# First expert of a fused attention and mixture kernel: its first 256 tokens in plain float32, weights unsplit

## The chip, the cores and the metric

One core of one Trainium2 chip runs the whole kernel in one launch. The metric is the device time of one execution in microseconds (us); a kernel's time is the median of its runs. The core has a matrix engine (TensorE, PE in the rows; PEld is its weight load), VectorE (DVE), ScalarE (ACT) and GpSimd (POOL); SyncE (SP) issues nearly all DMAs. Each engine works through its own queue in the order in which the program has it.

## The reference, cut to what matters

```python
# attention: q, k, v (2, 8, 576, 64); s (2, 8, 576)
scores = q @ k.T / 8;  bias = -(cum[:, None] - cum[None, :]),  cum = cumsum(max(s, 0))
attn = softmax(where(causal, -1e9, scores + min(bias, 0)))
x = (attn @ v), heads side by side             # 1152 tokens x 512
# four experts, every token goes through all of them
p = domain_probs / (domain_probs.sum(-1) + 1e-9)
x2 = sum over e of p[:, e] * (max(x @ w1[e], 0) @ w2[e])      # w1 512x1024, w2 1024x512
out = ((x2 @ w_a) * (x2 @ w_b)) @ w_out                        # 512 -> 1536 -> 512
```

All inputs and the output are float32.

## The kernel before

Products of two float32 matrices are made from halves: each operand is cut into a part hi in the engine's one-pass format (float32r) and a rest lo, and `mm3` (L260) adds hi*hi, hi*lo and lo*hi in three matmuls. So everything that goes into `mm3` has to be split first. For the weights `split_piece` (L194) does this: one DMA brings half a slab (128x1024, 512 KB) into one of three buffers called raw, one instruction copies it to wh, which rounds it, and two subtracts make wl. Two such pieces are a slab (a w1 or w2 block of 512x512), and an expert has four slabs: two of w1 and two of w2. The wh and wl of four slabs have a place at a time. `nsplit` counts pieces: for the first `NFIRST` = 4 the wh copy and both subtracts run on POOL; from the fifth on the wh copy runs on ACT (L220) and the subtracts (L222) alternate between POOL and DVE.

Attention runs in four groups of query rows. Group 0 is tokens 0 to 255 of the first batch, 8 heads of two 128-row tiles; its matmuls are plain float32 (L604, L692). The other groups use split halves. `attn_step` (L805) is a software pipeline over (head, tile): scores (L604, or L606 and L607), softmax (L617 on DVE, L632 on ACT), normalising (L644, on DVE for group 0 and on POOL later), transposing on PE (L655), copying the transposed tile from PSUM (L671 on ACT, from group 1 on also the rest el, L673 on DVE), attention times v (L692). For group 0 the result of two heads goes from PSUM straight to xh (ACT) and xl (DVE), L706.

The experts' products on tokens 0 to 767 stand beside the attention. `stages` (L865) holds expert 0 on the first 256 tokens, expert 1 on the same, then expert 1 on the next two blocks of 256. A stage has 8 first-layer units (12 matmuls of 256 columns, then relu to hh on ACT, L296, and the rest hl on DVE, L297) and 2 second-layer units (24 matmuls of 512 columns, then the weighted sum on DVE, L315 or L317). `advance` (L1096) paces attention steps against the estimated matmul time of the units, so that group 1 is done 15 us of estimate before the second stage ends. While group 0 runs, no product has begun; the loop at L1049 puts a weight step (one load, one split) after every second attention step. Everything after the attention (plain_stage, relu_stage, ab_stage) is not touched.

A scheduler puts the instructions of each engine in order. SP's order matters as well: a raw load waits there until its buffer is free, and whatever is queued behind it waits too, among it the key and query loads of the next heads (kr L558, qr L557, and kb L573, which sends a rounded key from ks back to another place).

```python
        else:                                             # split_piece, a slab's piece (L212)
            nsplit[0] += 1
            lo_eng = nc.gpsimd if nsplit[0] % 2 or nsplit[0] <= NFIRST else nc.vector
            two = slice(2 * j, 2 * j + 2)
            if nsplit[0] <= NFIRST:
                nc.gpsimd.tensor_scalar(                  # wh, L216
...
    while state["n"] < ends[0]:                           # L1049
        attn_step()
        if state["n"] > 3 and state["n"] % 2 == 0 and pieces:
            weight_step()
```

Of the kernel before, what the change touches and what calls it, by code (L numbers as in the profile page):

```python
# [8 lines left out]
F32 = mybir.dt.float32  # L9
F32R = mybir.dt.float32r  # L10
I32 = mybir.dt.int32
AF = mybir.ActivationFunctionType
ALU = mybir.AluOpType
# [32 lines left out]
NTT = NT // P  # L46
NT0 = 256

NFIRST = 4

LAG = 2

# [2 lines left out]
def fused_kernel(ctx, tc, qT, kT, v, s, dp, w1, w2, wa, wb, wo, out):  # L55
# [476 lines left out]
    first["v"] = vx[:, : H * 2 * D].rearrange("p (h c d) -> p h c d", h=H, c=2)  # L532
    NR = len(GROUPS) * H
    cum = vx[:NR, H * 2 * D :]
    ckr = slab.tile([P, 3 * S], F32R, tag="wh", name="ckr")
    ck3 = [ckr[:NR, j * S : j * S + S] for j in range(3)]

    def load_first(a, z, k_eng):
        for key, src, eng in (("q", qT, nc.sync), ("k", kT, k_eng)):
# [140 lines left out]
    def st_av(j):  # L680
        a = (j.h % 2) * D
        if j.gi == 0 and j.h % 2:
            ps = xpair[j.gi]
        else:
            ps = ps_a.tile([P, j.nr], F32, tag="av", name=f"av{j.nm}")
        mms = []
        for c in range(j.i1):
            o = max(0, j.tiles[c][1] - j.r0)
            for e in (j.eh, j.el) if j.gi else (j.eh,):
                mms.append((c, o, e))  # L690
        for m, (c, o, e) in enumerate(mms):
            ins = nc.tensor.matmul(  # L692
                ps[:, o:] if j.gi else ps[a : a + D, o:],
                lhsT=j.vs[:, c, :],
                rhs=e[:, c, o:],
                start=(m == 0),
                stop=(m == len(mms) - 1),
            )
        passed[-1].append(ins.ins.name)
        c = D - a  # L700
        t0 = j.b * S + j.r0
        x = slice(t0, t0 + j.nr)
        if j.gi == 0:
            xpair[j.gi] = ps
            if j.h % 2:
                split(xh[j.h // 2][:, x], xl[j.h // 2][:, x], ps, nc.vector)  # L706
            return
        if j.h % 2 == 0:
            xpair[j.gi] = (
                x_p.tile([P, j.nr], F32, tag="xs", name="xs"),  # L710
                x_p.tile([P, j.nr], F32, tag="xt", name="xt"),
            )
        xs, xt = xpair[j.gi]
        nc.scalar.activation(out=xt[a : a + D, :], in_=ps[c : c + D, :], func=AF.Copy)
        nc.vector.tensor_tensor(
            out=xs[a : a + D, :], in0=ps[a : a + D, :], in1=xt[a : a + D, :], op=ALU.add
        )
        if j.h % 2 == 1:
            split(xh[j.h // 2][:, x], xl[j.h // 2][:, x], xs, nc.gpsimd)
# [141 lines left out]
                queue((key, w), "slab", src[w])  # L861
        return ws

    halves = [queue_expert(ex) for ex in range(2)]
    stages = [(ex, halves[ex], *TURNS[0]) for ex in range(2)]  # L865
    stages += [(1, halves[1], *turn) for turn in TURNS[1:-1]]

    lasts = [(ex, m) for ex in (0, 2, 3) for m in range(2 * NPR)]
    for k, (ex, m) in enumerate(lasts):
# [16 lines left out]
    def pipelined(stages, last_ahead):  # L886

        units, pend = [], []
        for st, after in zip(stages, [*stages[1:], None]):
            if st is None:  # L890
                units += pend
                pend = []
                continue
            first_, second = st
            n = 1 if after or not last_ahead else len(first_)
            units += first_[:n] + pend + first_[n:]
            pend = second
        return units + pend

    def expert_stage(ex, ws, t0, t1):  # L900
        l1 = [
# [146 lines left out]

    while state["n"] < ends[0]:  # L1049
        attn_step()  # L1050
        if state["n"] > 3 and state["n"] % 2 == 0 and pieces:
            weight_step()

    def keys_of(k):
        return () if k is None else k if isinstance(k[0], tuple) else (k,)

    beside = pipelined([expert_stage(*st) for st in stages], False)
    after = pipelined(
        [plain_stage(w, m, *TURNS[-1]) for w in halves[1] for m in range(NPR)]
        + [relu_stage(ex, m) for ex, m in lasts]  # L1060
# [20 lines left out]
        area.append(area[-1] + (x[0].tiles[x[1]][0] + P if x else P))  # L1081

    turn_t = [0.0]
    for n in (2, 3, 4):
        us = sum(c for st in stages[:n] for part in expert_stage(*st) for _, c, _ in part)
        turn_t.append(us)
    SLACK = 15.0
    lead = []
    for g in range(3):
# [89 lines left out]
```

## Time and profile before

| | us |
|---|---|
| runs | 747.41, 751.63, 753.83 |
| median | 751.63 |
| the profiled execution's own time | 750.41 |
| its span, first to last instruction | 748.7 |
| mean granted TensorE clock | 0.990 of full speed |

The span is what the trace shows; the 1.7 us around it are the start and the end of the execution. Windows and start times count from the span's start. The profile gives the granted clock of PE as a share of 2.4 GHz, so 0.50 is the lower level, 1.2 GHz.

### The profile page before, as it was taken

To read this page: it belongs to the slowest core of one execution; us is meant where nothing else is said; L and a number is where in the kernel's file an instruction comes from. 1 tells how busy PE (TensorE), PEld (TensorE's weight loads), DVE (VectorE), ACT (ScalarE), POOL (GpSimd) and SP (SyncE) were. 2 spreads that over 40 slices of the span, in tenths; PEclk is the share of its full clock that TensorE was granted. 3 is DMA by queue.
4 is the path that set the end of the run, shared out by engine and by line. 5 is a ranking of instruction groups with operands and counts; after the bars stand their busy time and mean duration, and the time that the engine had idled before them with its cause. 6 is when DMAs were issued, how large, how long until landed. Compare 5 with 4: busy or idle time off the path is not lost.

```text
span 748.7 us, 11078 instructions
## 1 busy us (share of the span) xinstructions
PE 711.3 (95%) x3868; PEld 624.1 (83%) x3868; DVE 532.7 (71%) x1119; ACT 335.3 (45%) x756; POOL 413.4 (55%) x330
## 2 busy tenths in 40 slices
PE   5878889999999999999999999999899999999997
PEld 3567778898889888888888888887788888888886
DVE  7777688785777786666555656779783888877764
ACT  4577779986723432223231234333545434242410
POOL 1796676765513653333330356587468688798600
PEclk9889999999999999999999999999999999999999
DMA  6465523453220211111110113223013232223003
GB/s 182 158 211 175 148 73 104 110 139 92 55 85 29 85 56 57 57 56 57 57 39 18 57 57 85 65 77 111 28 43 99 59 90 79 85 72 97 1 1 127
DMA packets 35096, 61.34 MB, mean 82 GB/s; under 512 B 3473, under 2 KB 19377, under 8 KB 35041
## 3 DMA queue, kind: packets, MB, share of 16 engines
q1 hardware_dynamic: 34864, 60.50, 26.9%
q8 instruction: 31, 0.51, 0.3%
q14 instruction: 25, 0.20, 0.1%
q10 hardware_dynamic: 176, 0.14, 0.1%
HBM read 55.02 MB, written 2.58 MB: 77 GB/s over the span
## 4 chain that ended last, share of the span: by engine, by line
PE 59%; DVE 15%; POOL 9%; ACT 6%; issue 6%; DMA 4%; SPq 0%; POOLq 0%; ACTq 0%; DVEq 0%
PE ps L264 29%; PE psq L264 20%; PE pst L264 4%; POOL wl L76 3%; PE av L692 2%; PE tr L655 2%; DMA kr<-in_kT 2%; PE sc L604 1%; ACT e L632 1%; POOL tp L157 1%; DMA raw<-in_w 1%; DVE tp L169 1%; DVE tp L165 1%; DVE h2l L76 1%; ACT wh L220 1%
## 5 line engine op out<-in xcount | busy, mean ns | idle before, releaser
L264 PE MATMUL ps<-wh,h2h 128*128 128x512 f32 x332 | 130.6, 393 | 0.0
L264 PE MATMUL ps<-wl,h2h 128*128 128x512 f32 x332 | 129.6, 390 | 0.0
L76 POOL TENSOR_TENSOR wl<-raw,wh 128x1024 fp32r<-128x1024 f32 x24 | 58.2, 2434 | 128.3 <-ACT wh L75 97.9
L264 PE MATMUL ps<-wh,h2l 128*128 128x512 f32 x332 | 125.8, 392 | 0.8 <-DVE h2l L76 0.8
L317 DVE SCALAR_TENSOR_TENSOR acc<-ps,pr,acc 128x512 f32<-128x512 f32 x111 | 82.3, 745 | 40.4 <-PE ps L264 39.8
L264 PE MATMUL psq<-xh,wh 128*128 128x448 f32 (+1 forms) x224 | 81.6, 364 | 0.1
L264 PE MATMUL psq<-xl,wh 128*128 128x448 f32 (+1 forms) x224 | 81.2, 363 | 0.0
L264 PE MATMUL psq<-xh,wl 128*128 128x448 f32 (+1 forms) x224 | 81.2, 363 | 0.0
L264 PEld LDWEIGHTS ps<-wh,h2l 128*128 128x128 f32 x332 | 62.1, 188 | 14.8 <-DVE h2l L76 1.7
L264 PEld LDWEIGHTS ps<-wh,h2h 128*128 128x128 f32 x332 | 62.4, 188 | 11.8 <-ACT h2h L75 0.2
L328 ACT ACTIVATE h2h<-psq 128x448 fp32r<-128x448 f32 (+1 forms) x56 | 29.6, 532 | 93.9 <-PE psq L264 73.5
L264 PEld LDWEIGHTS ps<-wl,h2h 128*128 128x128 f32 x332 | 62.4, 188 | 11.1
L76 POOL TENSOR_TENSOR wl<-sums,wh 128x1024 fp32r<-128x1024 f32 x24 | 58.2, 2423 | 4.9 <-ACT wh L75 4.8
L75 ACT ACTIVATE wh<-raw 128x1024 fp32r<-128x1024 f32 x24 | 25.5, 1062 | 67.8 <-PE ps L264 51.7
L655 PE MATMUL tr<-ident,e 128*128 128x128 f32 x240 | 45.2, 289 | 11.0 <-DVE el L673 6.4
L264 PE MATMUL psq<-tqh,wh 128*128 128x448 f32 x144 | 52.9, 368 | 2.1 <-DVE u L415 1.3
L264 PE MATMUL psq<-tql,wh 128*128 128x448 f32 x144 | 52.6, 365 | 0.0
L264 PE MATMUL psq<-tqh,wl 128*128 128x448 f32 x144 | 52.5, 364 | 0.0
L644 POOL TENSOR_SCALAR e<-e,r 128x448 f32<-128x448 f32 (+4 forms) x64 | 37.9, 596 | 25.1 <-DVE r L643 23.1
L157 POOL TENSOR_SCALAR tp<-tp 128x512 f32<-128x512 f32 x24 | 47.3, 1988 | 6.5 <-ACT tp L156 6.5
L673 DVE TENSOR_TENSOR el<-tr,eh 128x512 fp32r<-128x512 f32 (+5 forms) x80 | 38.5, 483 | 16.1 <-ACT eh L671 15.4
L415 DVE TENSOR_TENSOR u<-psq,s 128x448 f32<-128x448 f32 x48 | 29.6, 618 | 28.4 <-PE psq L264 22.3
(174 smaller groups left out, 1963.3 us busy)
## 6 DMA issues: line engine op xcount, KB each, us to landing
raw<-in_w SPq DMA_DIRECT2D x40, 512.0 KB
raw<-in_wa SPq DMA_DIRECT2D x12, 512.0 KB
raw<-in_wb SPq DMA_DIRECT2D x12, 512.0 KB
raw<-in_wo SPq DMA_DIRECT2D x12, 512.0 KB
kr<-in_kT SPq DMA_DIRECT2D x16, 288.0 KB
vr<-in_v SPq DMA_DIRECT2D x16, 160.0 KB
kb<-ks SPq DMA_DIRECT2D x16, 144.0 KB
out<-acc SPq DMA_DIRECT2D x9, 256.0 KB
```

The costliest lines, as they stand in the source:

```text
L75: nc.scalar.activation(out=hi, in_=src, func=AF.Copy)
L76: lo_eng.tensor_tensor(out=lo, in0=src, in1=hi.bitcast(F32), op=ALU.subtract)
L157: nc.gpsimd.tensor_scalar(out=t.bitcast(F32), in0=t.bitcast(F32), scalar1=2.0**-15, scalar2=GMAX, op0=ALU.max, op1=ALU.min,)
L165: nc.vector.scalar_tensor_tensor(out=t, in0=lo, scalar=29, in1=t, op0=ALU.logical_shift_right, op1=ALU.bitwise_or,)
L264: ins = nc.tensor.matmul(ps, lhsT=l, rhs=r, start=first and k == 0, stop=last and k == 2, skip_group_check=more)
L317: nc.vector.scalar_tensor_tensor(out=dst, in0=ps, scalar=share, in1=dst, op0=ALU.mult, op1=ALU.add)
L328: nc.scalar.activation(out=hh, in_=src, func=AF.Relu)
L415: nc.vector.tensor_tensor(out=out, in0=a, in1=b, op=ALU.add)
L644: (nc.gpsimd if j.gi else nc.vector).tensor_scalar(out=t.e, in0=t.e, scalar1=r, scalar2=1.0, op0=ALU.mult, op1=ALU.mult)
L655: ins = nc.tensor.transpose(ps[:, c - c0, :], t.e[:, k0 : k0 + P], ident)
L673: nc.vector.tensor_tensor(out=j.el[:, c0:c1, x], in0=src, in1=hi.bitcast(F32), op=ALU.subtract)
L692: ins = nc.tensor.matmul(ps[:, o:] if j.gi else ps[a : a + D, o:], lhsT=j.vs[:, c, :], rhs=e[:, c, o:], start=(m == 0), stop=(m == len(mms ...
```

## The change

Expert 0's products on tokens 0 to 255 are no longer made from halves. `plain_expert` multiplies float32 by float32 in single matmuls (`mm1`): 8 first-layer units of 4 matmuls with 256 columns, and 2 second-layer units of 8 matmuls with 512. Its four weight blocks w32 are loaded as they are, after attention steps 4, 7, 11 and 15; each takes one place of the wh or wl kind, the two of w2 in places that others leave. x of group 0 is first copied by ACT from PSUM to x32, which lies in the buffer ckr, and split from there: xh on ACT, xl on POOL (DVE before). The relu of these units is one instruction, on ACT and DVE in turn, with no hl. The 8 pieces of expert 0's weights are not split any more. `NFIRST` is 0: the first pieces split are now expert 1's, with wh on ACT and the subtracts on POOL and DVE in turn. The pace counts 4 passes for a plain matmul, and the turns are counted without expert 0's old stage.

```diff
-NFIRST = 4
+NFIRST = 0
+
+W32_STEPS = (4, 7, 11, 15)
...
-    ckr = slab.tile([P, 3 * S], F32R, tag="wh", name="ckr")
-    ck3 = [ckr[:NR, j * S : j * S + S] for j in range(3)]
+    ckr = slab.tile([P, NC * SL], F32, tag="wh", name="ckr")
+    ck3 = [ckr[:NR, j * S : j * S + S].bitcast(F32R) for j in range(3)]
+    x32 = [ckr[:, o : o + NT0] for o in (3 * S, 0, NT0, 2 * NT0)]
+
+    w32 = {
+        (key, m): slab.tile([P, NC, SL], F32, tag=t, name="w32")
+        for key in ("w1", "w2") for m, t in enumerate(("wh", "wl"))
+    }
+
+    def load_w32(key, m):
+        src = {"w1": w1, "w2": w2}[key][m]
+        for two in (slice(0, 2), slice(2, 4)):
+            nc.sync.dma_start(out=w32[key, m][:, two, :], in_=src[:, two, :])
...
             if j.h % 2:
-                split(xh[j.h // 2][:, x], xl[j.h // 2][:, x], ps, nc.vector)
+                c_ = j.h // 2
+                nc.scalar.activation(out=x32[c_], in_=ps, func=AF.Copy)
+                split(xh[c_][:, x], xl[c_][:, x], x32[c_], nc.gpsimd)
...
-    halves = [queue_expert(ex) for ex in range(2)]
-    stages = [(ex, halves[ex], *TURNS[0]) for ex in range(2)]
-    stages += [(1, halves[1], *turn) for turn in TURNS[1:-1]]
+    halves = {1: queue_expert(1)}
+    stages = [(1, halves[1], *turn) for turn in TURNS[:-1]]
...
+    def mm1(ps, w, x, start, stop):
+        ins = nc.tensor.matmul(ps, lhsT=w, rhs=x, start=start, stop=stop)
...
+        if mixed:
+            mixed[0](4 * (x.shape[-1] / 2400 + 0.013))
+
+    def plain_expert():
+        h32 = {}
+        def first_(m, f):
+            ps = ps_m.tile([P, NT0], F32, tag="mm", name="ps1")
+            for c in range(NC):
+                mm1(ps, w32["w1", m][:, c, f * P : f * P + P], x32[c], c == 0, c == NC - 1)
+            h32[m, f] = h = pools["h"].tile([P, NT0], F32, tag="hh", name="h32")
+            if f % 2:
+                nc.vector.tensor_scalar(out=h, in0=ps, scalar1=0.0, scalar2=None, op0=ALU.max)
+            else:
+                nc.scalar.activation(out=h, in_=ps, func=AF.Relu)
+        def second(t):
+            ps = ps_m.tile([P, DM], F32, tag="mm", name="ps2")
+            for m in range(2):
+                for f in range(NF):
+                    mm1(ps, h32[m, f][:, t : t + P], w32["w2", m][:, f, :], m + f == 0, m == 1 and f == NF - 1)
+            add_share(ps, 0, t)
...
     while state["n"] < ends[0]:
         attn_step()
+        if state["n"] in W32_STEPS:
+            load_w32(*list(w32)[W32_STEPS.index(state["n"])])
...
-    beside = pipelined([expert_stage(*st) for st in stages], False)
+    beside = pipelined([plain_expert()] + [expert_stage(*st) for st in stages], False)
```

The line numbers of the changed program are 2 to 54 higher. Three places show how the order changes.

SP before, at the first weight loads: raw are pieces of expert 0's w1 (in_w1) and w2; qr, kr, kb, vr are loads of group 1's first heads, of which 0_2 is the first and 1_2 the second. Two more raw pieces of w1 stand ahead of these rows.

```order
L151 DMA raw_300<-in_w1 128x1024
L557 DMA qr0_0_2_389<-in_qT 128x384
L558 DMA kr0_0_2_390<-in_kT 128x576
L559 DMA kb0_0_2_391<-ckD_72 3x576
L559 DMA kb0_1_2_444<-ckD_72 3x576
L581 DMA vr0_0_2_464<-in_v 128x320
L151 DMA raw_340<-in_w1 128x1024
L557 DMA qr0_1_2_442<-in_qT 128x384
L573 DMA kb0_0_2_391<-ks0_0_2_435 64x576
L151 DMA raw_383<-in_w2 128x1024
L557 DMA qr0_2_2_500<-in_qT 128x384
L151 DMA raw_430<-in_w2 128x1024
```

SP of the change at the same place: w32_116 and w32_117 are the two halves of expert 0's w1; the raw pieces are now expert 1's.

```order
L550 DMA w32_116<-in_w1 128x1024 x2
L153 DMA raw_226<-in_w1 128x1024
L153 DMA raw_263<-in_w1 128x1024
L153 DMA raw_309<-in_w1 128x1024
L571 DMA qr0_0_2_401<-in_qT 128x384
L572 DMA kr0_0_2_402<-in_kT 128x576
L573 DMA kb0_0_2_403<-ckD_72 3x576
L573 DMA kb0_1_2_456<-ckD_72 3x576
L595 DMA vr0_0_2_476<-in_v 128x320
L550 DMA w32_117<-in_w1 128x1024 x2
L153 DMA raw_349<-in_w1 128x1024
L153 DMA raw_395<-in_w2 128x1024
```

The loads of the first head of group 1 now stand behind five pieces of 512 KB instead of three, and the second block of w1 comes straight behind them without a wait for a split. The two blocks of w2 are loaded much later, each into the place of a block of w1 that PE is done with.

ACT before, in the last heads of group 0: e0_5 to e0_7 are exponentials of heads 5 to 7, eh copies of transposed tiles, xh a result of group 0.

```order
L632 ACTIVATE e0_5_0_0_369,l_372<-e0_5_0_0_369,mn_370 128x128
L632 ACTIVATE e0_5_0_1_404,l_407<-e0_5_0_1_404,mn_405 128x256
L671 ACTIVATE eh0_4_0_379<-tr0_4_0_0_361 128x128
L567 ACTIVATE qh0_0_2_388<-qr0_0_2_389 128x384
L75 ACTIVATE xh_66<-av0_2_0_335 128x256
L632 ACTIVATE e0_6_0_0_419,l_422<-e0_6_0_0_419,mn_420 128x128
L671 ACTIVATE eh0_4_0_379<-tr0_4_0_1_395 128x2x128
L572 ACTIVATE ks0_0_2_435<-kr0_0_2_390 128x576
```

ACT of the change, from the same exponential on: wh_224 and wh_307 are slabs of expert 1, ckr_115 is x32.

```order
L646 ACTIVATE e0_5_0_0_380,l_383<-e0_5_0_0_380,mn_381 128x128
L222 ACTIVATE wh_224<-raw_226 128x1024
L646 ACTIVATE e0_5_0_1_416,l_419<-e0_5_0_1_416,mn_417 128x256
L685 ACTIVATE eh0_3_0_347<-tr0_3_0_1_354 128x2x128
L685 ACTIVATE eh0_4_0_391<-tr0_4_0_0_372 128x128
L646 ACTIVATE e0_6_0_0_431,l_434<-e0_6_0_0_431,mn_432 128x128
L222 ACTIVATE wh_224<-raw_263 128x1024
L646 ACTIVATE e0_6_0_1_469,l_472<-e0_6_0_1_469,mn_470 128x256
L721 ACTIVATE ckr_115<-av0_2_0_344 128x256
L685 ACTIVATE eh0_4_0_391<-tr0_4_0_1_407 128x2x128
L685 ACTIVATE eh0_5_0_440<-tr0_5_0_0_423 128x128
L222 ACTIVATE wh_307<-raw_309 128x1024
```

Three wh copies now stand between the exponentials of group 0; before, none did, since POOL made the first four.

DVE of the change, in heads 6 and 7 of group 0: the two subtracts of expert 1's second piece (wl_225) stand ahead of the normalising of head 6's second tile, e0_6_0_1; those of the fourth (wl_308) stand ahead of group 1's first softmax, e0_0_2_2. Before, DVE's first weight subtracts stood behind that softmax.

```order
L658 TENSOR_SCALAR e0_6_0_0_431<-e0_6_0_0_431,r_465 128x128
L645 TENSOR_SCALAR mn_532<-mn_532 128x1
L224 TENSOR_TENSOR wl_225<-raw_263,wh_224 128x512 x2
L654 TENSOR_SCALAR l_472<-l_472 128x1
L657 RECIPROCAL r_484<-l_472 128x1
L658 TENSOR_SCALAR e0_6_0_1_469<-e0_6_0_1_469,r_484 128x256
...
L658 TENSOR_SCALAR e0_7_0_1_531<-e0_7_0_1_531,r_548 128x256
L224 TENSOR_TENSOR wl_308<-raw_349,wh_307 128x512 x2
L582 SCALAR_TENSOR_TENSOR qb0_83<-qr0_1_2_454,qh0_1_2_453 64x384
L631 ISA e0_0_2_2_552,mn_553<-sc0_0_2_2_524,causal_82 128x320
```

DVE thus has two pairs of subtracts in or right behind group 0 that it did not have there, and fewer later.

PE's two orders are the same, buffer numbers aside, from just behind the scores of head 2's first tile in attention group 2 (sc_2_0_0, L606 and L607; the groups count from 0) to the end of the program: 3305 matmul instructions.

## Rows read from the trace of the kernel before

**Rows 1.** Windows: us of the stretch, busy us (instructions) by engine, granted clock, DMA share, GB/s.

```profile
0.00:36.20 36.20, 25.14 (x89) 15.44 (x89) 26.73 (x117) 17.76 (x58) 17.51 (x30) 0.92 0.54 164
36.20:98.50 62.30, 50.26 (x314) 45.27 (x313) 46.04 (x120) 48.77 (x127) 47.22 (x45) 0.94 0.56 170
98.50:122.00 23.50, 20.84 (x163) 19.51 (x163) 19.08 (x61) 18.58 (x60) 15.19 (x20) 1.00 0.34 95
122.00:748.70 626.70, 615.04 (x3307) 543.90 (x3306) 440.80 (x823) 250.19 (x512) 333.53 (x236) 1.00 0.23 68
```

**Rows 2.** Waits of PE from 0 to 140: us in total, times, longest.

```profile
PE sc L604 <- DMA ka<-va: 8.8, 1, 8.8
PE tr L655 <- DVE el L673: 6.0, 4, 2.0
PE sc L606 <- DVE mn L617: 3.0, 3, 1.5
PE sc L606 <- POOL ks L574: 2.6, 1, 2.6
PE sc L607 <- DMA kb<-ks: 1.3, 1, 1.3
```

**Rows 3.** Chain that ended last, 36 to 122, its shares by line.

```profile
by line: DMA raw<-in_w 10.8%; issue 10.4%; DMA kr<-in_kT 10.0%; PE ps L264 9.3%; ACT wh L220 8.1%; ACT e L632 6.4%; DVE wl L222 6.3%; PE av L692 4.4%; ACT eh L671 3.8%; POOL ks L574 3.5%; PE tr L655 3.5%; POOL wl L222 3.5%; DVE e L617 2.9%;
```

**Rows 4.** PE's timeline (start, us, instruction, count): plain float32 in group 0.

```profile
24.67 0.59 PE L604 MATMUL sc<-ka,qa 65*128 65x256 f32 x2
25.20 0.86 PE L692 MATMUL av<-eh,va 128*64 128x256 f32 x4
25.99 0.44 PE L655 MATMUL tr<-ident,e 128*128 128x128 f32 x2
```

**Rows 5.** Groups by shape of PE, 24.65 to 24.9: busy us, mean ns.

```profile
L604 PE MATMUL sc<-ka,qa 65*128 65x256 f32 x2 | 0.6, 378 | 0.0
```

**Rows 6.** PE's timeline: split products, 256 columns and 512 columns.

```profile
60.32 0.28 PE L264 MATMUL ps<-xh,wl 128*128 128x256 f32 x1
...
62.42 0.28 PE L264 MATMUL ps<-xh,wl 128*128 128x256 f32 x1
...
86.15 0.39 PE L264 MATMUL ps<-wl,hh 128*128 128x512 f32 x1
...
87.76 0.39 PE L264 MATMUL ps<-wh,hl 128*128 128x512 f32 x1
```

**Rows 7.** Instructions on raw, 0 to 122: ns min/median/max, first and last start.

```profile
L222 POOL TENSOR_TENSOR wl<-raw,wh x20: 1262/1334/1741, 20.0 to 100.2; 128x512 fp32r<-128x512 f32 x20
L220 ACT ACTIVATE wh<-raw x12: 1039/1051/1063, 36.6 to 102.0; 128x1024 fp32r<-128x1024 f32 x12
L222 DVE TENSOR_TENSOR wl<-raw,wh x12: 735/1406/1789, 38.7 to 103.8; 128x512 fp32r<-128x512 f32 x12
L216 POOL TENSOR_SCALAR wh<-raw x4: 1043/1048/1050, 18.9 to 31.4; 128x1024 fp32r<-128x1024 f32 x4
```

**Rows 8.** Groups of DVE and ACT from 0 to 122: rest and relu, busy us, mean ns.

```profile
L297 DVE SCALAR_TENSOR_TENSOR hl<-ps,hh 128x256 fp32r<-128x256 f32 x14 | 5.8, 412 | 1.1 <-ACT hh L296 0.9
L296 ACT ACTIVATE hh<-ps 128x256 fp32r<-128x256 f32 x14 | 5.2, 372 | 1.5 <-PE ps L264 1.5
```

**Rows 9.** Groups of POOL from 0 to 36.2, columns as in rows 8.

```profile
L222 POOL TENSOR_TENSOR wl<-raw,wh 128x512 fp32r<-128x512 f32 x6 | 7.9, 1338 | 0.1
```

**Rows 10.** DVE's timeline in group 0: the same normalising, POOL idle and POOL splitting.

```profile
18.04 0.35 DVE L644 TENSOR_SCALAR e<-e,r 128x256 f32<-128x256 f32 x1
...
30.23 1.25 DVE L644 TENSOR_SCALAR e<-e,r 128x256 f32<-128x256 f32 x1
```

**Rows 11.** Windows, columns as in rows 1: the last heads of group 0.

```profile
24.00:32.00 8.00, 6.32 (x31) 3.63 (x30) 7.47 (x30) 5.97 (x22) 7.83 (x7) 0.88 0.52 166
```

**Rows 12.** Instructions on kr up to 70, columns as in rows 7.

```profile
L572 ACT ACTIVATE ks<-kr x5: 672/683/687, 27.0 to 67.3; 128x576 fp32r<-128x576 f32 x5
```

**Rows 13.** Timeline of PE in head 1 of group 1: the longest wait there.

```profile
45.32 0.41 PE L606 MATMUL sc<-ks,qh 128*128 128x320 f32 x1 [2.60 <-POOL ks L574]
```

More of the change, by code (lines that the diff above doesn't have):

```diff
@@ L898, in pipelined @@
         return units + pend
+    def mm1(ps, w, x, start, stop):
+        ins = nc.tensor.matmul(ps, lhsT=w, rhs=x, start=start, stop=stop)
+        if len(passed) > LAG:
+            for name in passed[-1 - LAG]:
+                tc.add_manual_dep(ins.ins, name, NOSYNC, reason="the attention's pace")
+        if mixed:
[17 more added lines that the diff above has]
+            add_share(ps, 0, t)
+        T = 4 / 2400
+        l1 = [
+            (None, NC * (T * NT0 + 0.052), lambda m=m, f=f: first_(m, f)) for m in range(2) for f in range(NF)
+        ]
+        return l1, [(None, 2 * NF * (T * DM + 0.052), lambda t=t: second(t)) for t in range(0, NT0, P)]
     def expert_stage(ex, ws, t0, t1):
@@ L1083, in fused_kernel @@
     turn_t = [0.0]
-    for n in (2, 3, 4):
-        us = sum(c for st in stages[:n] for part in expert_stage(*st) for _, c, _ in part)
-        turn_t.append(us)
+    for n in (1, 2, 3):
+        parts = [*plain_expert(), *(part for st in stages[:n] for part in expert_stage(*st))]
+        turn_t.append(sum(c for part in parts for _, c, _ in part))
     SLACK = 15.0
```

## The prediction

> **What bounds the kernel now.** I read the busy time by stretch first, then PE's waits, then the chain of waits, then durations. In [rows 1] PE is busy 25.1 + 50.3 + 20.8 + 615.0 = 711.3 of 748.7 us, so PE bounds the kernel; the reader should see where the other 37.4 us lie: 11.1 before 36.2, 12.0 in the 62.3 us of expert 0's stage, 2.7 in the next 23.5, and 11.7 in all the 627 us behind. PE's order is the same in both programs from about 122 us on, so nothing behind that point has a reason to change: the change is decided in the first 122 us.
>
> Of the 25.8 us that PE waits there, 8.8 are for the operands of the first scores, which both programs need [rows 2]. The 14.7 us between 36.2 and 122 are mostly waits for DVE (rests of the transposed tiles 6.0, score buffers 3.0), POOL (2.6) and a key transfer (1.3). None is long, and no engine but PE is near full on average: DVE 46.0, ACT 48.8 and POOL 47.2 of 62.3. The chain tells what feeds the waits [rows 3]: of the 86 us from 36 to 122 its steps are raw loads 10.8%, wh copies 8.1%, subtracts on DVE 6.3% and on POOL 3.5%, together 28.7% or 24.7 us, and 10.0% are key loads, which stand on SP behind raw loads. PE's own products are 9.3%. So the splitting of expert weights sets the pace here, in queues that it shares with the attention. [Rows 13] is an example: PE waits 2.6 us for the rest of head 1's keys, which POOL makes after weight subtracts.
>
> **The change part by part.** *PE's products.* Taken away are 8 x 12 = 96 matmuls of 256 columns and 2 x 24 = 48 of 512. In [rows 6] 18 steps lie between 60.32 and 62.42, 0.117 us each, and seven between 86.15 and 87.76, 0.23 each: 96 x 0.117 + 48 x 0.23 = 11.2 + 11.0 = 22.2 us. Added are 32 plain matmuls of 256 columns and 16 of 512. A plain one is two records: two of 256 columns cover 0.59 us [rows 4] and are 0.378 long [rows 5], so the second starts 0.212 after the first. A product of 256 columns is then 0.425 us, and one of 512, with twice the columns, 0.85 (an estimate from this row): 32 x 0.425 + 16 x 0.85 = 13.6 + 13.6 = 27.2, **+5.0 us**. From above: the four records of 256 and 128 columns in [rows 4] take 25.20 to 25.99 = 0.79 where 1.5 x 0.425 = 0.64 would be due, 0.15 too much for two products; 0.075 on each of the 48 would be 3.6 more, +8.6. Those products have a pass of 128 columns; ours have none below 256, so I take the row of 256. From below: 0.212 is the spacing of passes without a gap, so nothing under +5.0 is left.
>
> *Splits that go.* Expert 0's four slabs were 8 of 16 pieces. From 36.2 to 122 the 12 wh copies on ACT [rows 7] fall to 4 (expert 1's third and fourth slab; the first two are now copied in group 0): 8 x 1.05 = 8.4 us less. DVE's 12 subtracts fall to 4, 8 x 1.4 = 11.2 less; POOL's 20 less the six before 36.2 [rows 9] fall from 14 to 4, 10 x 1.33 = 13.3 less. With the plain relu 8 rests on DVE and 4 relus on ACT go, and 4 plain ones on DVE come, at 0.41 and 0.37 us [rows 8]: 1.6 less on DVE, 1.5 on ACT. So DVE sheds 12.8 of 65.1 us (46.0 + 19.1), ACT 9.9 of 67.4, POOL 13.3 of 62.4. The 3.9 us of waits on keys should go, since the split in front of them is gone or earlier, and most of DVE's 9.0; PE also has 5 us more to do in the gaps. I take 10 of the 14.7 us as recovered: **-10 us**. The bounds are 0 (the waits are the softmax's own latency, and the new passes are laid beside them) and -14.7.
>
> *Splits that are moved into group 0.* ACT gets three wh ahead of the last exponentials, 3 x 1.05 = 3.2, and two copies to x32, 0.8 by the 256-column pass of [rows 8]. In 24 to 32 ACT has 8.0 - 6.0 = 2.0 us free [rows 11], so 2.0 of the 4.0 is late. DVE gets two subtracts ahead of head 6's normalising, 2 x 1.4 = 2.8, and gives three xl to POOL, 3 x 0.41 = 1.2. In return DVE runs faster: a normalising takes 0.35 us with POOL idle and 1.25 with POOL splitting [rows 10]. POOL's splits here fall from 4 x 1.05 + 7.9 = 12.1 us to 4 x 1.33 = 5.3, and at up to 0.9 for each normalising that they met I take 2 us as relief. Together 2.0 + 2.8 - 1.2 - 2.0 = **+1.6 us**, between -2 (the copies hidden, the relief kept) and +6.8 (4.0 + 2.8, nothing hidden).
>
> A rule speaks against this term. [Rows 7] show DVE's subtract at 0.735 us at best and 1.41 in the median. The Trainium skill ("SBUF — State Buffer", Who interferes with whom) says that a DVE instruction with two SBUF inputs contends with a GpSimd instruction that reads SBUF, and that the shared port is an exclusive lock. By it, DVE's two subtracts in group 0, now beside POOL's, would cost up to 0.735 + 1.26 = 2.0 us each, 4.0 instead of 2.8, and the sum would be 1.2 us higher; the spread of the row agrees in kind.
>
> *Loads.* The first head's keys stand behind 1 MB more on SP, 6 us at the first stretch's 164 GB/s [rows 1]; ACT first rounds them at 27.0 [rows 12]. Hidden, unless they landed after 21. The last block of w2 is loaded only when the first layer is done, again 6 us; in front of its first use PE has 12 split products (1.4 us), four plain ones (3.4) and attention matmuls. Cost nothing; if that cover is short, 1 to 4 us.
>
> *The clock.* The granted clock is 0.92 and 0.94 in the first two stretches [rows 1]; between the levels of 0.5 and 1 that is some 6 and 7 us at the lower one. I take it as unchanged, with 2 us either way in the range.
>
> **Sum**: 750.4 + 5.0 - 10 + 1.6 = 747.0 for the profiled execution, which lies 1.2 us below the median of the runs shown; so **748.2** as a median, 3.4 us faster.
>
> **Rivals.** 1. *All waits go.* PE becomes the only bound of the stage, and group 0 gets no longer: 750.4 + 5.0 - 14.7 = 740.7, 741.9 as a median. For it: every other engine drops to about two thirds of the stage or less. Against it: PE waits 2.7 us even in 98.5 to 122, where few splits are left, and the softmax has a latency of its own.
>
> 2. *Early splits hold up the softmax* (slower than before). Three wh on ACT and a pair of subtracts on DVE now stand between the exponentials and normalisings of heads 5 to 7, and the first scores of group 1 and all products wait behind them. The full price is 6.8 us: 750.4 + 5.0 + 6.8 - 10 = 752.2, 753.4 as a median. It decides from 5 us of delay on, where the recovered waits are used up. For it: DVE is busy 7.5 of the 8 us from 24 to 32 [rows 11]. Against it: ACT is not, and POOL's relief comes at the same time.
>
> 3. *The waits stay.* If PE's gaps are the latency of scores, exponential, transposing and rest through in-order queues, and the splits only filled the others' free time, the plain passes are just more work: 750.4 + 5.0 + 1.6 = 757.0, 758.2 as a median; with 3.6 of exposed weight loads 761.8. Against it: over a quarter of the chain is splitting.
>
> 4. *The change doesn't do what it says*: the weights, unsplit, are still waited for, because w2 is loaded late into the places of w1. With 4 us for that the forecast becomes 752.2.
>
> **How the numbers follow.** Forecast 0.5, rival 1 0.17, rival 2 0.18, rival 3 0.12, rival 4 0.03. A measurement of this kernel tells about 1%, 7.5 us, from no change; the bounds are 744.1 and 759.1. Faster by over 1%: most of rival 1 (0.15) and the lucky end of the forecast, all waits but 2 us gone (0.05): 0.20. Slower: rival 3 with exposed loads or more delay (0.07) and rival 2 with less recovered (0.03): 0.10. Within: 0.70. The range for 8 in 10 goes from rival 1's 741.9, rounded down, to rival 3's 758.2.
>
> **What would show it.** Right: plain products at 0.42 to 0.43 us with 256 columns and 0.85 with 512; PE idle for about 5 us instead of 14.7 between the first scores of group 1 and the common point; that point, now at 122, about 3.4 us earlier; everything behind it as long as before; the DVE rests and the key transfer gone from the top of PE's waits; group 1's first scores within 2 us of their 36.2. Wrong: a plain product of 0.5 us or more; group 1's first scores 5 us late, with DVE or ACT splits ahead of heads 6 and 7 (rival 2); the same waits on rests and scores with the splits gone (rival 3); a wait of PE for w32 (rival 4); or a changed length behind the common point, on which no term rests.

## The result, and the profile after

The changed kernel takes 743.28 us (median of 4 runs, 738.71 to 744.0) against 751.79 for the kernel before in the same job (4 runs): 0.9876 of it, 95% interval 0.9835 to 0.9917, so faster by about 1.2%. The profiled execution took 743.07 us, its span 741.3.

The windows of the changed kernel (columns as in [rows 1]) are cut at group 1's first scores, the end of expert 0's stage, and the common point, from which PE's order is the same in both programs. In the traces that point is not quite "just behind the scores of head 2". In the kernel before, the common order begins with one product of attention and v behind those scores, at 122.09 us. In the changed kernel eight such products and a transpose, which ran ahead of the scores before, still stand behind them, and the common order begins at 115.82. From there to the end both traces have the same 3304 matmuls.

```profile
0.00:37.49 37.49, 25.56 (x79) 15.65 (x79) 26.18 (x115) 21.13 (x63) 11.75 (x25) 0.98 0.60 196
37.49:96.04 58.55, 56.41 (x292) 44.12 (x292) 40.73 (x122) 44.09 (x126) 36.87 (x41) 0.96 0.55 170
96.04:115.82 19.78, 18.98 (x150) 17.80 (x148) 17.25 (x50) 15.54 (x54) 13.39 (x17) 1.00 0.27 74
115.82:741.30 625.48, 615.37 (x3306) 545.69 (x3305) 440.50 (x823) 249.43 (x512) 333.45 (x236) 1.00 0.21 68
```

The kernel before, cut at its own common point:

```profile
122.09:748.70 626.61, 614.95 (x3306) 543.81 (x3305) 440.71 (x823) 250.19 (x512) 333.53 (x236) 1.00 0.23 68
```

So 6.3 of the 7.4 us that the span lost lie ahead of the common point, which came at 115.8 in place of 122.1. The other 1.1 lie behind it, where PE's order is the same: in the thirteen traces (with the runs below) that have these 3304 matmuls in the same order they take 624.4 to 627.7 us. Between the first scores and the common point PE was idle for 14.7 of 85.9 us before; now it is 78.33 - 56.41 - 18.98 = 2.9 of 78.3.

PE's waits from 0 to 140, columns as in [rows 2]:

```profile
PE sc L618 <- DMA ka<-va: 8.6, 1, 8.6
PE tr L669 <- DVE el L687: 2.9, 5, 1.5
PE av L706 <- ACT eh L685: 2.3, 3, 1.9
PE sc L620 <- POOL ks L588: 1.1, 1, 1.1
```

The waits on mn and on the key transfer are gone, those on rests are halved, the one on ks fell from 2.6 to 1.1. None is on w32. New is the wait of av on eh, 2.1 of its 2.3 us ahead of the first scores.

The instructions on raw pieces from 0 to 122, columns as in [rows 7]:

```profile
L222 ACT ACTIVATE wh<-raw x8: 1037/1047/1064, 22.9 to 89.8; 128x1024 fp32r<-128x1024 f32 x8
L224 POOL TENSOR_TENSOR wl<-raw,wh x8: 1263/1300/1777, 24.1 to 97.9; 128x512 fp32r<-128x512 f32 x8
L224 DVE TENSOR_TENSOR wl<-raw,wh x8: 679/1074/1757, 31.4 to 98.5; 128x512 fp32r<-128x512 f32 x8
```

Half the pieces, as the change says; four of the eight wh copies start ahead of the first scores (at 22.9, 27.2, 30.9 and 36.0).

The plain products: first the records that read w32 (ns min/median/max), then two stretches of PE's timeline.

```profile
L918 PE MATMUL ps<-ckr,w x64: 377/379/635, 41.0 to 67.0; 128*128 128x256 f32 x64
L918 PE MATMUL ps<-w,h x32: 592/592/596, 69.6 to 96.0; 128*128 128x512 f32 x32
```

```profile
44.62 2.75 PE L918 MATMUL ps<-ckr,w 128*128 128x256 f32 x12
...
77.04 2.74 PE L918 MATMUL ps<-w,h 128*128 128x512 f32 x6
```

Twelve records cover 2.75 us and one is 0.379 long, so they start (2.75 - 0.379) / 11 = 0.216 apart: 0.43 a product of 256 columns. For 512 columns it is (2.74 - 0.592) / 5 = 0.43, or 0.86 a product.

Set beside each other, the 122.1 and the 115.8 us are:

| us | before | after | change |
|---|---|---|---|
| PE busy to the first scores | 25.1 | 25.6 | +0.4 |
| PE idle to the first scores | 11.1 | 11.9 | +0.9 |
| PE busy from there to the common point | 71.2 | 75.4 | +4.2 |
| PE idle there | 14.7 | 2.9 | -11.8 |

The first scores are not the end of group 0. In the kernel before, its last product of attention and v ends at 36.25, ahead of every product of the experts; in the changed kernel two heads' products stand behind the first scores (rows at 38.42 and 43.18 in the last section). The first product of an expert begins at 41.02 in place of 37.63.

### The profile page after: what moved, and what is told of

The parts are those of the page before. It is cut to its first block, busy times and chain, and to the rows that moved or that the text cites. A ratio compares the mean times of both kernels' runs of the same rounds, so it can differ in the third digit from the quotient of the medians.

```text
span 741.3 us, 10949 instructions
## 1 busy us (share of the span) xinstructions
PE 716.3 (97%) x3820; PEld 623.3 (84%) x3820; DVE 524.7 (71%) x1107; ACT 330.2 (45%) x752; POOL 395.5 (53%) x318
## 4 chain that ended last, share of the span: by engine, by line
PE 64%; DVE 15%; POOL 9%; issue 5%; ACT 4%; DMA 3%; POOLq 0%; SPq 0%; ACTq 0%; DVEq 0%
PE ps L266 29%; PE psq L266 20%; PE pst L266 4%; PE av L706 3%; POOL wl L78 3%; PE tr L669 3%; PE ps L918 2%; DMA kr<-in_kT 2%; PE sc L618 1%; POOL tp L159 1%; DVE tp L171 1%; DVE tp L167 1%; DVE h2l L78 1%; DVE acc L1093 1%; DVE tp L163 1%
## 5 line engine op out<-in xcount | busy, mean ns | idle before, releaser
L266 PEld LDWEIGHTS ps<-wh,h2h 128*128 128x128 f32 x332 | 62.4, 188 | 11.7 <-ACT h2h L77 0.3
L266 PE MATMUL psq<-tql,wh 128*128 128x448 f32 x144 | 52.7, 366 | 0.0
L646 ACT ACTIVATE e<-e,mn 128x128 f32<-128x128 f32 (+4 forms) x80 | 45.7, 572 | 9.3 <-DVE mn L631 7.4
```

The source lines that it names most:

```text
L266: ins = nc.tensor.matmul(ps, lhsT=l, rhs=r, start=first and k == 0, stop=last and k == 2, skip_group_check=more)
L646: nc.scalar.activation(out=t.e, in_=t.e, func=AF.Exp, bias=mn, scale=-1.0 if j.gi else -SCALE, accum_out=t.l)
```

## The experiments

Ratios are to the kernel before, run in the same job. "Stretch" is from group 1's first scores to the common point (85.9 us with 14.7 idle before, 78.3 with 2.9 after; the expectations cut the changed kernel just behind head 2's scores, at 114.6, and so say 77.1). Where a window of PE is shown its columns are those of [rows 1].

**The splits put back, products plain.**

```diff
+    spare = [(j, k) for k in range(4) for j in range(2)]
+    def spare_split(j, k):          # called first by weight_step, until 8 are done
+        n = 2 * k + j
+        t = pools["raw"].tile([P, 2, SL], F32R, tag="raw", name="spare")
+        src = w32["w1", 0][:, 2 * j : 2 * j + 2, :]
+        # n < 4: copy on POOL, else on ACT; two subtracts on POOL or DVE
```

> The changed kernel (743.3 us) with the splitting work of expert 0's eight pieces put back: same copies and subtracts, same engines as before (the first four pieces on POOL, then wh on ACT and subtracts on POOL and DVE in turn), reading the unsplit w1 and writing to a raw buffer that nobody reads; the output stays the reference's. No byte more is loaded, PE's products stay plain. Theory A (the splits' work in the queues of ACT, DVE and POOL made PE's waits): PE idle between group 1's first scores and the common point goes from 2.9 back to 9 to 15 us, time 749 to 756. Rival B (the plain products, longer and without a rest to wait for, cover the latency by themselves; the splits only filled free time): idle stays at 2 to 5, time 742 to 746.

759.65 us, 1.0078 (1.0048 to 1.0107): 2% or some 15 us above the changed kernel, and slower than before. The stretch, and PE's and DVE's longest waits in it:

```profile
38.88:132.50 93.62, 77.22 (x430) 63.00 (x429) 65.26 (x176) 66.02 (x184) 58.83 (x64) 0.95 0.42 124
```

```profile
PE sc L636 <- DVE mn L647: 11.3, 4, 6.9
PE sc L637 <- DMA kb<-ks: 2.4, 1, 2.4
...
DVE spare L248 <- ACT spare L245: 6.4, 2, 4.7
```

PE idles 16.4 us again. So the plain products do not cover the waits by themselves (B falls). The size is more than A said: four spare pieces came bunched, and two of DVE's stood for 6.4 us waiting for their copies, ahead of the first softmax of group 1. The spare pieces also take the first eight weight steps, so that expert 1's own pieces stand behind eight others, as before the change: their first wh copy starts at 51.5 us in place of 22.9. What the chain costs and what that delay costs are not told apart here, and the size is an upper bound. The kernel lies 5.9 us above the kernel before; the prediction priced plain products with the splits' waits kept at 758.2.

**Expert 0's subtracts left out, products split.**

```diff
-            for m in (2 * j, 2 * j + 1):
+            for m in (2 * j, 2 * j + 1) if nsplit[0] > 8 else ():
...                                     # expert 0's products read wh in place of wl
```

> The kernel before (751.8 us) with expert 0's eight weight pieces loaded and copied to wh as before, but without their 16 subtracts; its products stay three matmuls and read wh in place of wl, so the rests of expert 0's weights are left out of the output. Theory A: about half of the splits' engine time is gone (POOL 12 x 1.3 and DVE 4 x 1.4 us), raw buffers come free earlier; PE idle from 36 to 122 falls from 14.7 to 5 to 9 us, time 743 to 748. Rival B (waits go by the form of the products): idle 12 to 15, time 750 to 753.

Four executions: 738.48 (the profiled one), 749.58, 750.38 and 751.3, too far apart for a time. In the profiled one the stretch was 84.95 us with 8.7 idle, at the upper end of A. But its first scores came at 26.85, with the clock at the higher level from 18 us on (in the changed kernel from 32, last section), and the other three executions lie in B's range or just under it. So this run speaks for neither theory.

**NFIRST = 4 in the changed kernel.**

```diff
-NFIRST = 0
+NFIRST = 4
```

> The changed kernel with the first four pieces split on POOL alone, as before (they are expert 1's now). The prediction's third term (early splits on ACT and DVE cost 1.6 us): group 1's first scores at about 36 in place of 37.5 us, time 741.5 to 742.5. Rival C (POOL holds those scores up: in the changed kernel they wait for the rest of the keys, which stands behind two weight subtracts on POOL; with wh on POOL too it stands behind more): first scores at 38.5 to 42, time 744 to 748.

746.36 us, 0.9928 (0.9898 to 0.9959), 3 to 4 us above the changed kernel (by the medians and by the ratios); the intervals overlap. First scores at 37.9, so nothing was gained there, nor lost as C had it, though the time is in C's range.

```profile
37.88:118.30 80.42, 74.38 (x429) 60.89 (x429) 56.41 (x168) 58.72 (x174) 53.37 (x61) 0.98 0.49 143
```

The stretch is 2.1 us longer, with 6.0 us idle in place of 2.9. All of group 0's products of attention and v stand ahead of the first scores here, so PE has less to do behind them. The price came behind the first scores, a place that neither expectation named.

**NFIRST = 0 in the kernel before.**

```diff
-NFIRST = 4
+NFIRST = 0
```

> The kernel before with its first four pieces split like the others (wh on ACT, subtracts on POOL and DVE in turn), which is one part of the change alone. The prediction's third term: group 1's first scores 1 to 2 us later than 36.2, time 752 to 754. Rival D (this part is itself a gain, since POOL's queue is freed and the later splits start earlier): first scores no later, waits from 36 to 122 below 13 us, time 747 to 750.

754.92 us, 1.0026 (0.9996 to 1.0056): up to 0.6% slower or no change. This part alone gives nothing, so D falls. The first scores came early, at 33.0, but four heads' products of attention and v of group 0 still stood behind them, at 36.5, 39.3, 46.0 and 52.7, and the stretch took 94.5 us with 13.8 idle. In this execution PE also stayed at the lower clock longer than in any other here: the product at 46.0 still took 1.54 us, the one at 52.7 took 0.86. So the time of the first scores alone is a poor measure of group 0's length.

**Spare work on one engine at a time.** The changed kernel, each with one of the three loops.

```diff
+    def spare_work(j):              # once for each head of group 1
+        a, b = j.ks[:, :SL].bitcast(F32), j.ks[:, S - SL :].bitcast(F32)
+        for _ in range(2):          # ACT
+            nc.scalar.activation(out=t, in_=a, func=AF.Copy)
+        for _ in range(1):          # DVE
+            nc.vector.tensor_tensor(out=t, in0=a, in1=b, op=ALU.subtract)
+        for _ in range(1 + (j.h < 2)):  # POOL
+            nc.gpsimd.tensor_tensor(out=t, in0=a, in1=b, op=ALU.subtract)
```

> The changed kernel with 8 spare subtracts of 128x512 on DVE, one per head of attention group 1 (reading that head's keys, writing a tile that nobody reads): the 11 us that DVE shed. If the waits went because DVE's queue was freed (before, 10.2 of the 14.7 us of PE's waits ended on DVE): 747 to 752, 4 to 8 above the changed kernel, PE waits on el or mn. If DVE's share was filling (the run before put back all splits, bunched, and cost 15): within 2 of the changed kernel.

> The changed kernel with 8 spare copies of 128x1024 on ACT (as 16 of 128x512), two per head of group 1: the 8.4 us that ACT shed. If the wh copies in front of exponentials and eh made the waits: 746 to 750, PE waits on ACT or on DVE rests behind eh. If DVE's queue alone did: within 2 of the changed kernel.

> The changed kernel with 10 spare subtracts of 128x512 on POOL in the heads of group 1: the 13.3 us that POOL shed. If POOL's queue made waits by the keys' rests and by slowing DVE's two-input work beside it: 745 to 749, with a wait of PE on POOL ks. If POOL has room: within 2 of the changed kernel.

DVE: 741.89 us, 0.987 (0.9814 to 0.9926). ACT: 743.46, 0.9881 (0.9826 to 0.9936). POOL: 744.13, 0.9884 (0.9823 to 0.9945). None differs from the changed kernel's 0.9876. The three stretches, in this order:

```profile
37.52:115.47 77.95, 75.19 (x438) 61.79 (x439) 62.93 (x179) 60.15 (x180) 53.44 (x57) 0.97 0.49 146
```

```profile
37.45:116.02 78.57, 75.40 (x439) 61.86 (x439) 57.93 (x171) 67.85 (x195) 50.27 (x57) 0.97 0.48 145
```

```profile
31.86:109.97 78.11, 75.51 (x438) 62.02 (x439) 58.99 (x171) 60.57 (x180) 63.26 (x67) 0.96 0.49 146
```

PE's idle time stays at 2.6 to 3.2 us, with 5.0 us more on DVE, 8.2 on ACT and 13.0 on POOL. (DVE's spare subtracts took 0.76 us each, so 6.1 and not the 11 us that were meant.)

**Spare work on all three.**

```diff
+        for _ in range(3):
+            nc.scalar.activation(out=spare_t[0], in_=a, func=AF.Copy)
+        for _ in range(2):
+            nc.vector.tensor_tensor(out=spare_t[1], in0=a, in1=b, op=ALU.subtract)
+            nc.gpsimd.tensor_tensor(out=spare_t[2], in0=a, in1=b, op=ALU.subtract)
```

> The changed kernel with all three kinds of spare work at once, spread over the heads of group 1 (per head three copies of 128x240 on ACT, two subtracts of 128x240 each on DVE and POOL: about 8 x 1.1, 8 x 1.0 and 8 x 1.4 us), without the chain from copy to subtract and without raw buffers. Theory A (engine time in the queues makes the waits): 750 to 756, PE idle between group 1's first scores and the common point 9 to 14 in place of 2.9. Rival (what cost 15 us in the run with the splits put back was their chain over raw buffers, bunched ahead of the first softmax): 744 to 748.

747.19 us, 0.9924 (0.9893 to 0.9955), some 4 us above the changed kernel.

```profile
37.53:119.56 82.03, 77.44 (x439) 63.50 (x439) 65.51 (x187) 66.64 (x203) 64.40 (x73) 0.95 0.47 139
```

All three engines are about as busy as before the change ([rows 1]: 65.1, 67.4 and 62.4 us from 36.2 to 122), and PE idles 4.6 us, not 14.7. So engine time is a small part of the 11.8 (1.7 us); the rival's range is met. What this kernel lacks beside the one with the splits put back is the chain (load, copy, subtract, buffer), its bunching, and the delay of expert 1's own pieces.

**Split products without splits of their own.**

```diff
+    slabs.update({(k, m): slabs["w1", 2] for k in ("w1", "w2") for m in range(2)})
+    split0 = [[(None, *u[1:]) for u in part] for part in expert_stage(0, (0, 1), *TURNS[0])]
-    beside = pipelined([plain_expert()] +
+    beside = pipelined([split0] +
...                                     # the pace counts split0 in plain_expert's place
```

> The changed kernel with expert 0's products made from halves again, three matmuls each, but without splits of its own: the halves of expert 1's first block stand in as its weights, so expert 0's part of the output for the first 256 tokens is left out of what the time tells; its unsplit weights are still loaded. PE's work falls by the 5.0 us of the prediction's first term, and 8 rests come back on DVE. If the waits went because the split chain of eight pieces is gone: PE idle between group 1's first scores and the common point stays at 2 to 5, that stretch 72 to 75 in place of 77.1, time 737 to 741. If they went because the plain products are longer and need no rest: idle 9 to 14, stretch 80 to 84, time 745 to 750.

738.55 us, 0.9814 (0.9757 to 0.9871), where the first theory had it and 4.7 below the changed kernel.

```profile
33.52:111.60 78.08, 72.30 (x483) 66.44 (x481) 58.41 (x178) 61.73 (x183) 47.45 (x56) 0.93 0.44 127
```

PE idles 5.8 us, between the two expectations and nearer the first. By these profiles, one execution of each, 14.7 - 5.8 = 8.9 of the 11.8 us that the change won back go with the splits alone, and the other 2.9 with the form of the products. The stretch is longer than expected, with a granted clock of 0.93: 2 x 0.07 x 78.1 = 11 us at the lower level against 2 x 0.03 x 78.3 = 5 in the changed kernel. The early first scores need not be an effect of the products: the clock rose at 17 us in this execution, as in the one with spare work on POOL, whose first scores came at 31.86.

**The subtracts one step later, in the kernel before.**

```diff
-            for m in (2 * j, 2 * j + 1):
-                lo_eng.tensor_tensor(...)
+            rests.append((key, rest))   # rest() holds that loop; weight_step calls it first
```

> The kernel before with the same splits on the same engines, but from the fifth piece on the two subtracts of a piece are given out one weight step after its wh copy, so that DVE and POOL no longer stand and wait for ACT's copy (before: 4.4 and 4.7 us from 36 to 122). If engines blocked in order by the split chain made PE's waits: PE idle from 36 to 122 falls from 14.7 to 8 to 11, time 746 to 750. If it is the chain's length through the three raw buffers and SP's order (key loads behind raw loads): raw buffers are held longer, waits on keys grow, time 752 to 757.

751.93 us, 0.9988 (0.996 to 1.0017): no change. But the edit did not take away what it was to take away: from 36 to 122 DVE still stood 4.1 us and POOL 6.6 for ACT's wh (4.4 and 4.7 before). PE's waits, 38.31 to 124.6:

```profile
PE tr L672 <- DVE el L690: 5.5, 4, 2.1
PE sc L623 <- POOL ks L591: 4.5, 1, 4.5
```

Whether standing behind the copy makes PE's waits stays open.

**Work for PE ahead of the first scores.**

```diff
+    warm = ps_m.tile([P, NT0], F32, tag="mm", name="warm")
+    for k in range(7):
+        nc.tensor.matmul(warm, lhsT=ones[:, :P], rhs=ones[:, :NT0], start=k == 0, stop=k == 6)
```

> The changed kernel with seven plain matmuls of 256 columns on a tile of ones, ahead of the first scores, in the 8.6 us in which PE waits for the first loads; their result is not read. In the profiled executions PE ran at the lower of its levels from its first matmul until 17 to 36 us (four plain matmuls of attention times v take 1.54 us there, 0.86 behind it). If work ahead of the first scores lets the clock rise earlier: the 0.86 us rows begin at 10 to 17 us, group 1's first scores at 32 to 35, time 735 to 740. If not: 743 to 745, as the changed kernel.

743.58 us, 0.9881 (0.9832 to 0.9931): as the changed kernel. PE's timeline, and two windows:

```profile
7.77 0.59 PE L757 MATMUL warm<-ones 128*128 128x256 f32 x2
...
10.14 0.49 PE L618 MATMUL sc<-ka,qa 65*128 65x128 f32 x2 [0.66 <-DVE mn L631]
11.83 1.65 PE L618 MATMUL sc<-ka,qa 65*128 65x256 f32 x4 [1.20 <-DVE mn L631]
```

```profile
7.50:10.90 3.40, 2.27 (x10) 1.20 (x9) 1.31 (x5) 2.27 (x3) 0.00 (x0) 1.00 0.60 168
10.90:41.60 30.70, 27.48 (x82) 17.86 (x83) 20.39 (x102) 18.97 (x61) 11.92 (x16) 0.50 0.61 209
```

The clock rose ahead of the first scores, but it did not stay. The last two records on the tile of ones cover 0.59 us, as two records of 256 columns do at the higher level ([rows 4]), and two records of 128 columns cover 0.49 at 10.14, where the changed kernel's took 0.64 at 13.68. Then PE waited 0.66 and 1.20 us for DVE, and from 10.9 to 41.6 us the clock is at the lower level. So no row of 0.86 us came early. The first expectation fails not at the rise but at what it took for granted, that the higher level lasts.

**The first splits eight attention steps later.**

```diff
-        if state["n"] > 3 and state["n"] % 2 == 0 and pieces:
+        if state["n"] > 11 and state["n"] % 2 == 0 and pieces:
```

> The changed kernel with its first weight step after attention step 12 in place of 4, so that only the last pieces are split in group 0. The prediction's third term (early splits on ACT and DVE hold group 0 up by 1.6 us): group 1's first scores at 34 to 36.5, time 740 to 742. If the early splits are free there and the later ones meet the attention: first scores within 1 of 37.5, idle behind them 5 to 8, time 745 to 749.

750.14 us, 0.9952 (0.9926 to 0.9979): 6 to 7 us above the changed kernel, so most of the gain is lost by the place of a few pieces. PE's longest waits from 30 to 121.25 us, and what POOL does ahead of the first scores:

```profile
PE av L706 <- ACT eh L685: 3.1, 4, 1.3
PE sc L620 <- POOL ks L588: 2.8, 1, 2.8
```

```profile
35.02 2.81 POOL L224 TENSOR_TENSOR wl<-raw,wh 128x512 fp32r<-128x512 f32 x2 [0.22 <-ACT wh L222]
37.90 1.40 POOL L588 TENSOR_TENSOR ks<-kr,ks 64x576 fp32r<-64x576 f32 x1
```

A split begun at 35 stands in front of the keys' rest, and the first scores come at 39.35 in place of 37.5. Behind them PE idles 7.6 of 83.1 us. The first expectation falls: first scores and time both came later. Of the second only the idle time is in its range; the scores came 1.9 us later, where 1 was given, and the time is 1 us above. Still, its direction holds: the splits cost less in group 0 than beside group 1. Group 0 itself was done sooner, its last product of attention and v ending at 36.5 in place of 44.0. No kernel here that computes the whole reference was measurably faster than the changed one.

## Why the prediction was right, and which terms were off

Direction, place and range were right: 748.2 was forecast, 743.3 came, inside 741.5 to 758.2. The gain was 2.5 times the forecast one, 8.5 us of the median in place of 3.4, and close to rival 1, in which all waits go. The sum for the profiled execution was +5.0 - 10 + 1.6 = -3.4. In the same order the tables above give +4.6 (busy time, 0.4 + 4.2), -11.8 (idle behind the first scores) and +0.9 (idle ahead of them), and -1.1 behind the common point: -7.4.

*PE's products, +5.0.* Right for the plain ones: 0.43 and 0.86 us, as forecast. The profiles show 4.6 us more PE work, but the near agreement has luck in it. "0.117 us each" is wrong for 24 of the 96 products taken away, which ran at the lower clock in the profile of before. PE's timeline there, the second and the last of each twelve:

```profile
37.84 0.42 PE L264 MATMUL ps<-xl,wh 128*128 128x256 f32 x1
...
39.98 0.41 PE L264 MATMUL ps<-xh,wl 128*128 128x256 f32 x1
...
54.39 0.41 PE L264 MATMUL ps<-xl,wh 128*128 128x256 f32 x1
...
56.52 0.41 PE L264 MATMUL ps<-xh,wl 128*128 128x256 f32 x1
```

Ten steps take 2.14 and 2.13 us, 0.213 each; 24 x (0.213 - 0.117) = 2.3 us more were taken away than counted. On the other side, group 0 ran at the lower level until 32 us in the changed kernel's execution and until 23 in that of before (last section). Whether the 4.6 us count on the path in full is not shown. The kernel with split products has a median 4.7 us lower, with overlapping intervals; but in its trace the common order begins at 111.58, and in that with spare work on POOL, where the clock rose at the same 17 us and the products are plain, at 109.97. (The clock of the former also fell to the lower level again from 48 to 55 us.)

*The clock.* "Some 6 and 7 us at the lower one" was read from the granted clock of [rows 1]. By the length of its matmuls PE also ran at the lower level from its first matmul to 23 us, where the column reads 1.00 (last section). The 2 us either way in the range are too few for that: the execution with the rise at 17 us lies 5.8 us and more below the others of its kernel (last section).

*Waits recovered, -10.* Mis-sized, at 11.8 of 14.7, and its reason only partly right. "The splitting of expert weights sets the pace" holds: put back, it brought 16.4 us of idle time, and without it even split products idle only 5.8. But the working counted the time that each engine sheds, and engine time is not what PE waited for: 5 to 13 us on any one engine cost nothing, on all three together some 4 us. Engines also shed less than counted, DVE 65.1 - 58.0 = 7.1 us for 12.8. What is left is the chain of a piece and its place in the queues: eight pieces fewer also bring expert 1's pieces forward, and undoing part of that (the first splits eight attention steps later) cost 6 to 7 us by itself. No run put the chain back without that delay, so the two are not told apart, nor is it settled which link counts most (the three raw buffers with SP's order, or the copy and subtract in front of a softmax). Rival 3, that splits only fill free time, is refuted.

*Splits moved into group 0, +1.6.* The first scores came 1.3 us later, inside the 2 us given. That is no clean measure of the term: two heads' products were left behind those scores, and the clock rose at 32 us in place of 23; in the run with spare work on POOL, where it rose at 17, the first scores came at 31.86. As a cost of group 0 the term is borne out in kind, since without the early splits group 0's last product ended at 36.5 in place of 44.0. But they save more behind: split on POOL alone (NFIRST = 4), the kernel is 3 to 4 us slower, with overlapping intervals; with the splits later, 6 to 7. The engines named were DVE and ACT. ACT is borne out: PE's longest wait ahead of the first scores, 1.88 us, is for its copies eh, which stand on ACT behind a wh copy and the rounding of group 1's first queries, keys and values (from 30.89 to 34.36). POOL was not named: the first scores wait 1.1 us for its rest of the keys, and the chain of waits from 30 to 40 us (start, length) leads there through ACT's wh copy and POOL's subtracts:

```profile
31.00 0.94 ACT wh L222
...
34.14 0.93 POOL wl L224
35.07 0.69 POOL xl L78
...
35.84 1.60 POOL ks L588
```

DVE's first two subtracts in group 0 took 0.68 us each where 1.4 was counted (the group of the first 37.4 us: busy us, mean ns, idle before):

```profile
L224 DVE TENSOR_TENSOR wl<-raw,wh 128x512 fp32r<-128x512 f32 x2 | 1.3, 684 | 0.0
```

The row gives 1.37 us for both. They started at 31.39 and 31.99; POOL's timeline at that place:

```profile
32.02 3.05 POOL L224 TENSOR_TENSOR wl<-raw,wh 128x512 fp32r<-128x512 f32 x2 [5.46 <-ACT wh L222]
```

The rule from the Trainium skill ("SBUF — State Buffer", Who interferes with whom), by which DVE's would have cost up to 2.0 each, was hardly put to the test: POOL had stood idle for 5.46 us and began behind DVE's second. It was POOL's pair that took longer, 3.05 us beside 2.49 for the pair at 24.07.

*Loads.* Right: PE never waits for w32. Behind the larger queue the first keys were rounded at 33.4 in place of 27.0, but ACT came to that copy without a wait.

*Behind the common point*: 1.1 us shorter, where no change was forecast; with the same order of matmuls and a spread of 3.3 us among the traces, nothing shows that the change did it. Rival 2 did not happen, and rival 4 neither.

## What to carry to other kernels

Removing a helper chain (load, convert, subtract, free a buffer) from in-order queues can give more than the busy time it sheds suggests: price it by the waits behind it, and test it by putting back engine time and chain separately, without moving other work. Where such a chain must stay, its place counts: eight attention steps cost 6 to 7 us here. Put it early, where the engines that run it have time to spare (in group 0 here, where PE itself was the limit for a while), and look at what stands behind it in each queue, such as a softmax or the keys. And do not take the first instruction of the next part for the end of the last one: compare programs from where their orders agree. And read the matrix engine's clock from the length of equal instructions before using a duration for a stretch.

## What the runs showed of the hardware

The clock of PE in group 0 was not what the window's column says. One head's two plain products of attention and v, four records of 256 and 128 columns, take 1.54 us at the lower level and 0.86 at the higher. In the profile of before:

```profile
19.55 1.54 PE L692 MATMUL av<-eh,va 128*64 128x256 f32 x4
23.44 0.86 PE L692 MATMUL av<-eh,va 128*64 128x256 f32 x4
...
30.46 1.54 PE L692 MATMUL av<-eh,va 128*64 128x256 f32 x4
```

In that of the changed kernel:

```profile
30.89 1.54 PE L706 MATMUL av<-eh,va 128*64 128x256 f32 x4 [0.26 <-ACT eh L685]
34.78 0.86 PE L706 MATMUL av<-eh,va 128*64 128x256 f32 x4 [1.88 <-ACT eh L685]
38.42 1.54 PE L706 MATMUL av<-eh,va 128*64 128x256 f32 x4
43.18 0.86 PE L706 MATMUL av<-eh,va 128*64 128x256 f32 x4
```

And with spare work on POOL, whose first spare subtract starts at 33.2:

```profile
15.76 1.50 PE L706 MATMUL av<-eh,va 128*64 128x256 f32 x4
18.33 0.86 PE L706 MATMUL av<-eh,va 128*64 128x256 f32 x4
...
29.55 0.86 PE L706 MATMUL av<-eh,va 128*64 128x256 f32 x4 [2.56 <-ACT eh L685]
32.79 1.54 PE L706 MATMUL av<-eh,va 128*64 128x256 f32 x4
```

The clock rose at about 23, 32 and 17 us, although the column gives this window of the changed kernel, in which PE was never idle and ran at the lower level, as 1.00:

```profile
12.00:24.00 12.00, 12.00 (x37) 7.68 (x37) 8.33 (x58) 7.98 (x30) 2.13 (x8) 1.00 0.90 305
```

So PE itself bounded group 0 from 12 to 24 us. The clock fell again at about 30, 36 and 31 us, each time soon after a wait of PE: 1.68 us for DVE before, 1.88 and 2.56 for ACT in the other two. The early rise brought group 1's first scores to 31.86 in place of 37.5, with the stretch behind unchanged (78.1 us beside 78.3), and that execution took 738.25 us where the other three of the same kernel took 744.05 to 745.19. The changed kernel's 738.71 beside 743.07 to 744.0 is of the same size, but its trace was not taken. Matmuls ahead of the first scores brought a rise at 7.5 us, which was lost again at 10.9, behind two short waits of PE. What decides when the clock first rises, and how long that lasts, was not found.

The Trainium skill ("TensorE: Matmul & The Clock Gate", Seeing it yourself) warns that the trace's clock events are not to be trusted alone; the trace here agrees, with 1.00 in the row above where the matmuls ran at half pace.
